# Sorted block attention and an affine MLP on one core: k mixed in four row tiles, the Sinkhorn steps dealt differently, x written by blocks on three queues, W2 loads moved, the last output tile in column halves

## The chip, the cores and the metric

The kernel runs on one core of one Trainium2 chip. The metric is the time of one execution in device microseconds (us). The kernel before ran three times: 330.39, 331.08 and 332.67 us, median 331.08 us.

## The reference

There are two stages. The first is an attention within blocks, whose keys and values are first mixed over blocks by a matrix P that comes from a Sinkhorn iteration; the second is a residual MLP.

```python
# q, k, v: (4, 8, 768, 64); sort_net: (4, 8, 8, 8); a block has 96 rows
P = sort_net
for _ in range(5):
    P = P - np.max(P, axis=-1, keepdims=True)
    P = np.exp(P)
    P = P / (np.sum(P, axis=-1, keepdims=True) + 1e-09)
    P = P / (np.sum(P, axis=-2, keepdims=True) + 1e-09)
k_sorted = np.einsum('bhij,bhjcd->bhicd', P, k_b)     # the same for v
scores = scale * np.matmul(q_b, k_sb.transpose(0, 1, 2, 4, 3))
attn = softmax(scores)
x = heads_side_by_side(np.matmul(attn, v_sb))         # (4, 768, 512)

a1 = alpha1 * x + beta1
tok = np.einsum('ts,bsd->btd', w_tok, a1)
u = x + lam * tok
a2 = alpha2 * u + beta2
out = u + lam * (np.maximum(a2 @ w_ch1, 0.0) @ w_ch2) # hidden size 2048
```

## The kernel before

The four batches go through attention and then through the MLP. The order of all instructions on every engine is the order in which the Python code emits them (a manual schedule); each engine takes its own in that order, and semaphores hold it where data or a buffer is missing. The interleaving is done by generators: each `yield` gives a cost, and `run(gen, n)` lets a generator emit n more pieces.

PSUM is two pools, `psS` and `psM`, of two buffers each. A buffer that is still to be read is not given out again, so where one of the two is held, the other serves alone.

**Front.** `sinkhorn(0)` normalises P of batches 0 and 1, `sinkhorn(1)` that of 2 and 3; each iteration is an exp with row sums on ScalarE (ACT), a reciprocal and a product on VectorE (DVE), a matmul for the column sums on TensorE (PE, L197) into a psS buffer, and again a reciprocal and a product. `big_p` turns P into the weights of the mixing matmuls (L222 to L228). `q_path(b)` transposes q on PE (L360) and copies it out (L369). `mix_k(b)` makes the mixed and transposed k: one small matmul for each of the 96 rows of a block and each group of heads (L265). In batches 0 and 1 a matmul uses 32 of the array's rows and 64 of its columns, and two row groups take turns; in batches 2 and 3, which are done together, it uses 64 rows. Every 32 matmuls fill one PSUM tile, which `evict_k` copies out on ACT (L240) or DVE (L242).

**Attention of a batch.** `scores_max` computes the scores once for the row maxima (PE L393, DVE L399), transposes the maxima (L413) and spreads them on a diagonal Dt (L418). `heads` computes the scores again with the maximum taken off (L436, L444), the exp ET on ACT (L451), the product with v (L461), and the normalised rows in `xnat` on DVE (L470, L471). `bounce` writes x to `xscr` in DRAM, one half of the rows (four blocks) at a time, and `read` reads it back as `x16` with token rows in the partitions:

```python
        def bounce(g):
            t0 = g * S // 2
            n = BLK // NT
            dst = xscr[b, t0:t0 + S // 2].rearrange("(i s k) c -> k s i c", s=n, k=NT)
            for kk in range(NT):
                eng = nc.scalar if b == 0 and g == 1 and kk % 2 else nc.sync
                eng.dma_start(dst[kk], xnat[kk * n:(kk + 1) * n, g * 4:(g + 1) * 4])
```

**MLP of a batch.** `tok_mix` has six token tiles; each has six matmuls of 128 x 512 (L531), a product on DVE (L537), an add to u on GpSimd (POOL; for odd tiles of batch 0 on DVE, L539) and a cast to bf16 on ACT (L543). `u_transposes` turns three tiles of u on PE (L559) and scales them into `a2T` on ACT (L568) and DVE (L573). `ch1` is the first channel matmul (L588, eight per step), with a relu on ACT (L598) or DVE (L596); `ch2` the second (L607), with a product on DVE (L614), an add on POOL (DVE for the last batch, L616) and the write of the output from SyncE (SP, L617).

**Order between the two.** Batch 0's attention runs alone; then `mixing()` emits the MLP of all batches, and between its pieces the loop at the end of the code lets `attention()` emit pieces of the later batches, as long as a credit lasts that each MLP piece adds to. POOL's queue issues the loads of q, k, v and the weights (`load_q`, `load_halves`, `load_23`, `load_w1`, `load_w2`). The second half of W1 is held back by a small copy, the gate (L717), until batch 0's second x16 is there. SP's queue issues the writes and reads of x, v and the output.

Of the kernel before, what the change touches and what calls it, by code (L numbers as in the profile page):

```python
# [9 lines left out]
FT = mybir.dt.float32  # L10
# [9 lines left out]
def kernel(  # L20
# [160 lines left out]
    def sinkhorn(n):  # L181
        P = sortP[n]
        rs = wt([128, 1], FT, f"rs{n}")
        c8 = wt([128, NB], FT, f"c8{n}")

        top = wt([128, 1], FT, f"top{n}")
        nc.vector.tensor_reduce(top[:], P[:], AXX, ALU.max, negate=True)
        for it in range(5):
            if it == 0:
                nc.scalar.activation(P[:], P[:], AF.Exp, bias=top[:], accum_out=rs[:])  # L190
            else:
                nc.scalar.activation(P[:], P[:], AF.Exp, accum_out=rs[:])
            yield
            nc.vector.reciprocal(rs[:], rs[:])
            nc.vector.tensor_scalar(P[:], P[:], rs[:], None, op0=ALU.mult)
            cs = ps2(psS)
            nc.tensor.matmul(cs[:, 0, 0:NB], blkf, P[:], start=True, stop=True)  # L197
            yield
            if it == 0:

                nc.vector.tensor_scalar(c8[:], cs[:, 0, 0:NB], 1e-9, None, op0=ALU.add)
                nc.vector.reciprocal(c8[:], c8[:])
            else:
                nc.vector.reciprocal(c8[:], cs[:, 0, 0:NB])
            nc.vector.tensor_tensor(P[:], P[:], c8[:], ALU.mult)

        BD = BD_of[n] = wt([128, 16, NB], F16, f"BD{n}")
        nc.vector.tensor_tensor(
            BD[:], P[:].unsqueeze(1).to_broadcast([128, 16, NB]),
            mask_blk[:].unsqueeze(2).to_broadcast([128, 16, NB]), ALU.mult,  # L210
        )
        yield
# [20 lines left out]
    def kT_tile(b):  # L233

        kT_of[b] = at([128, H4 * NB, BLK], F16, "kT", 2)

    def evict_k(b, cols, t16):
        dst = kT_of[b][:, :, t16 * 16:(t16 + 1) * 16].rearrange("p c (b t) -> p c b t", b=2)
        if t16 % 2 == 0:
            nc.scalar.copy(dst, cols)  # L240
        else:
            nc.vector.tensor_copy(dst, cols)  # L242

    def mix_k(b, pools):
        raw = raw_of["k", b]
        both = (b, b + 1) if b == 2 else (b,)
        for b_ in both:
            kT_tile(b_)
        w = 32 * len(both)
        for t16 in range(BLK // 16):  # L250
            ps = ps2(pools[t16 % len(pools)])
            for turn in range(2):
                for tt in range(8):

                    for hl in range(2):
                        bank = (hl + turn) % 2
                        t = t16 * 16 + bank * 8 + tt
                        if b == 2:
                            r = slice(hl * 64, hl * 64 + 64)
                            P = PT_of[1][r, r]  # L260
                        else:
                            th, t = divmod(t, BLK // 2)
                            r = slice(th * 64 + hl * 32, th * 64 + hl * 32 + 32)
                            P = PT_of["k"][r, b, hl * 32:hl * 32 + 32]
                        nc.tensor.matmul(  # L265
                            ps[hl * 64:hl * 64 + 64, bank, tt * w:(tt + 1) * w],
                            raw[r, t * D:(t + 1) * D], P,
                            start=True, stop=True,
                        )
            cols = ps[:, :, 0:8 * w].rearrange("p b (t c) -> p c b t", c=w)  # L270
            for n, b_ in enumerate(both):
                evict_k(b_, cols[:, n * 32:n * 32 + 32], t16)
            yield 1.2

    def vS_tile(b):
# [104 lines left out]

    D_of = {}

    def scores_max(b):

        mx = at([BLK, 2, H4, NB], FT, "mx", 1)
# [22 lines left out]
        mxf = mx[:].rearrange("p l h i -> p l (h i)")  # L408
        nc.vector.tensor_copy(mh[:, :, 0, :], mxf)
        nc.vector.tensor_tensor(mh[:, :, 1, :], mxf, mh[:, :, 0, :], ALU.subtract)  # L410
        yield 0.6
        tp = psS.tile([128, 2, 1024], BF, name="m_ps", tag="psS")
        nc.tensor.transpose(  # L413
            tp[:, 0, 0:BLK], mh[:].rearrange("p l e c -> p (l e c)"), identbf[0:BLK, 0:BLK]
# [1 line left out]
        for g in range(2):  # L416
# [2 lines left out]
                Dt[:], tp[:, 0, 0:BLK].unsqueeze(1).to_broadcast([128, 4, BLK]),  # L419
                mask_j[:, g * 4:(g + 1) * 4].unsqueeze(2).to_broadcast([128, 4, BLK]), ALU.mult,  # L420
            )
        yield 1.0

    x16_of = {}

    def heads(b, xpool):
# [50 lines left out]
            )  # L477

        def bounce(g):
            t0 = g * S // 2  # L480
            n = BLK // NT
            dst = xscr[b, t0:t0 + S // 2].rearrange("(i s k) c -> k s i c", s=n, k=NT)
            for kk in range(NT):
                eng = nc.scalar if b == 0 and g == 1 and kk % 2 else nc.sync
                eng.dma_start(dst[kk], xnat[kk * n:(kk + 1) * n, g * 4:(g + 1) * 4])

        def read(g):
            t0 = g * S // 2
# [36 lines left out]
    def tok_mix(b):  # L525
        u = u_of[b]
        u16 = u16_of[b] = mt([128, NT, C], BF, "u16", 1)
        for kt in range(NT):
            ps = ps2(psM)
            for ks in range(NT):  # L530
                nc.tensor.matmul(  # L531
                    ps[:, 0, :], w_tokT[ks][:, kt * 128:(kt + 1) * 128],
                    x16_of[b, ks // 3][:, ks % 3, :],
                    start=(ks == 0), stop=(ks == NT - 1),
                )
            tmp = mt([128, C], FT, "tmp", 2)
            nc.vector.tensor_tensor(tmp[:], ps[:, 0, :], a1lB[:], ALU.mult)  # L537
            eng = nc.vector if b == 0 and kt % 2 else nc.gpsimd
            eng.tensor_tensor(u[:, kt], u[:, kt], tmp[:], ALU.add)  # L539
            if b == 0 and kt < 3:  # L540
                add_x0(kt + 3)
            if kt > 0:
                nc.scalar.copy(u16[:, kt - 1], u[:, kt - 1])  # L543
            if b == 0 and kt > 0:
                load_w2(kt - 1)
            if kt == NT - 2:
                u_transposes(b, 0, psM if b == 0 else psS)
            yield 1.0
        nc.scalar.copy(u16[:, NT - 1], u[:, NT - 1])

    def u_transposes(b, half, pool):
# [49 lines left out]
    def ch2(b, half, k1):  # L601

        u, hT = u_of[b], hT_of[b, half]
        kt = half * 3 + k1
        ps = ps2(psM)
        for m in range(HT):
            nc.tensor.matmul(  # L607
                ps[:, 0, :], hT[m // 2][:, m % 2, k1 * 128:(k1 + 1) * 128],
                W2[:, m, :], start=(m == 0), stop=(m == HT - 1),
            )  # L610
            if m == HT // 2 - 1:
                yield 1.8
        tmp = mt([128, C], FT, "tmp", 2)
        nc.vector.tensor_tensor(tmp[:], ps[:, 0, :], lamB[:], ALU.mult)  # L614
        eng = nc.vector if b == B - 1 else nc.gpsimd
        eng.tensor_tensor(u[:, kt], u[:, kt], tmp[:], ALU.add)  # L616
        nc.sync.dma_start(out[b, kt * 128:(kt + 1) * 128, :], u[:, kt])  # L617
        yield 1.8

    def tok_weights():  # L620
# [38 lines left out]


    vS_tile(0)
    sink, sink1, q0 = sinkhorn(0), sinkhorn(1), q_path(0, psS)
    run(sink, 4)
    nc.scalar.copy(ident16[:], ident32[:])
    run(sink1, 1)
    for it in range(3):
        run(sink, 1)
        run(sink1, 1)
        run(sink, 1)
        if it == 0:  # L670
            nc.scalar.copy(identbf[:], ident32[:])
        if it == 1:
            nc.vector.tensor_reduce(
                m4[:], mask_blk[:].rearrange("p (g h) -> p h g", h=H4), AXX, ALU.add
            )
            nc.scalar.activation(
                nsel[:], m4[:].unsqueeze(2).to_broadcast([128, H4, BLK]), AF.Identity, scale=-1.0
            )
        if it < 2:
            run(sink1, 1)  # L680
# [1 line left out]
    run(sink)  # L682
    big_p(0)
    run(q0, 1)
    mk0 = mix_k(0, [psM, psS])
    for n in range(6):
        run(mk0, 1)
        run(sink1, 1)
        if n == 0 or n == 2:
            run(q0, 1)  # L690
    run(q0)
    run(mk0)
    run(sink1)
    big_p(1)
    load_halves("k", k, 1)
    load_q(1)
    load_w1(0)
# [1 line left out]
        nc.gpsimd.tensor_tensor(dst[:], src[:], lamB[:], ALU.mult)  # L699

    top, mix, tokw = scores_max(0), mix_v0(psM), tok_weights()
    for _ in range(8):
        run(top, 1)
        run(mix, 1)
    run(top, 1)
    run(tokw, 2)
    run(top)
# [14 lines left out]

    def attention():
        yield from mix_v1(psS)
        yield from mix_k(1, [psS])
        yield from q_path(1, psS)
        yield from scores_max(1)
        yield from heads(1, psS)
        yield from mix_v23(psS)
        yield from mix_k(2, [psS])  # L730
        yield from q_path(2, psS)
        load_q(3)
        yield from scores_max(2)
# [3 lines left out]
        yield from heads(3, psS)  # L737

    att_ = attention()
    run(att_, 8)  # L740
    for kt in range(3):
        add_x0(kt)
    run(att_, 6)


    def mixing():

        for _ in tok_mix(0):
            yield 1.0
        for b in range(B):  # L750
            part = ch1(b, 0)
            yield next(part)
# [27 lines left out]
    for part in mixing():  # L780
        credit = min(credit + part, 3.0)
        while credit > 0.0:
            cost = next(att_, None)
            if cost is None:
                break
            credit -= cost
    run(att_)


# [28 lines left out]
```

## Time and profile before

| | |
|---|---|
| runs | 330.39, 331.08, 332.67 us |
| profiled execution: its own time | 333.6 us |
| profiled execution: span of its instructions | 331.8 us |
| mean granted TensorE clock | 0.963 |
| PE busy | 299.9 us (90%), 2926 matmuls |
| DVE, ACT, POOL busy | 156.0, 122.4, 100.6 us |
| L588 and L607 (the two channel matmuls) | 89.1 and 88.6 us |
| L531 (token mixing) | 36.3 us |

All durations come from the profiled execution; the span is what its instructions cover, and 1.8 us of its own time lie around that. A busy PE is not a PE at its peak, since matmuls overlap and the clock that the throttle grants can be half. "Idle before" in brackets at the end of a timeline row tells how long the engine waited and for whom. POOLq, SPq and ACTq stand for the issue of DMAs by those engines' queues.

### The profile page before, as it was taken

How to read it: one execution, taken by the hardware profiler on the slowest of the kernel's cores; microseconds unless marked ns; L12 is line 12 of the kernel's file. 1: busy time of each engine (PE TensorE's matmuls, PEld its weight loads, DVE VectorE, ACT ScalarE, POOL GpSimd, SP SyncE). 2: the span in 40 equal slices, each digit the busy share in tenths (PEclk: the TensorE clock that was granted, in tenths of full speed). 3: DMA queues.
4: the chain of work that ended last, by engine and by line, in shares of the span. 5: the costliest groups of instructions: out<-in, count | busy, mean ns of one | idle time of the engine just before them, and what ended most of it. 6: DMA issues, size and time to landing. Idle time of an engine off the chain costs nothing.

```text
span 331.8 us, 6817 instructions
## 1 busy us (share of the span) xinstructions
PE 299.9 (90%) x2926; PEld 177.7 (54%) x2926; DVE 156.0 (47%) x290; ACT 122.4 (37%) x190; POOL 100.6 (30%) x103
## 2 busy tenths in 40 slices
PE   2579888897899999987999999999999999999994
PEld 2469775743465456443566446645554545554641
DVE  5447663577645444863546844452111153123223
ACT  4324583313584265142354026342220524220400
POOL 8207100238221191641110118073204763300000
PEclk9999995587999999997999999999999999999999
DMA  7998926999999579900035013203101000101001
GB/s 104 200 216 200 207 38 149 204 162 148 222 213 171 129 302 137 152 1 32 34 81 145 3 62 79 49 5 125 63 2 63 33 2 32 63 2 63 32 34 63
DMA packets 39170, 33.35 MB, mean 101 GB/s; under 512 B 20836, under 2 KB 33892, under 8 KB 38692
## 3 DMA queue, kind: packets, MB, share of 16 engines
q0 software_dynamic: 9552, 15.60, 26.6%
q1 hardware_dynamic: 29348, 17.12, 22.7%
q8 instruction: 23, 0.38, 0.5%
q10 hardware_dynamic: 240, 0.20, 0.3%
q14 instruction: 7, 0.06, 0.1%
HBM read 35.93 MB, written 11.80 MB: 144 GB/s over the span
## 4 chain that ended last, share of the span: by engine, by line
PE 75%; DVE 9%; DMA 5%; ACT 4%; POOL 3%; issue 2%; DVEq 0%; ACTq 0%; POOLq 0%; SPq 0%
PE psM L607 25%; PE psM L588 24%; PE psM L531 4%; PE psS L461 3%; DMA W<-in_moe_w_ch_dram 3%; POOL u L539 3%; PE psS L436 3%; DVE mx L399 2%; PE psS L393 2%; PE q_ps L360 2%; PE psS L265 2%; DVE tmp L537 2%; PE psS L444 2%; ACT ET L451 1%; PE uT_ps L559 1%
## 5 line engine op out<-in xcount | busy, mean ns | idle before, releaser
L588 PE MATMUL psM<-a2T,W 128*128 128x384 bf16 x512 | 89.1, 326 | 0.4 <-ACT hT L598 0.3
L607 PE MATMUL psM<-W,hT 128*128 128x512 bf16 x384 | 88.6, 384 | 0.0
L598 ACT ACTIVATE hT<-psM 128x768 bf16<-128x768 f32 x48 | 38.9, 811 | 73.6 <-PE psM L588 73.5
L588 PEld LDWEIGHTS <-W 128*128 128x128 bf16 x512 | 48.2, 98 | 31.4 <-issue 0.7
L607 PEld LDWEIGHTS <-hT 128*128 128x128 bf16 x384 | 37.0, 99 | 42.2 <-issue 1.7
L616 POOL TENSOR_TENSOR u<-u,tmp 128x512 f32<-128x512 f32 x18 | 22.8, 1264 | 95.1 <-DVE tmp L614 95.1
L451 ACT ACTIVATE ET<-psS 96x768 f16<-96x768 f32 x32 | 25.5, 804 | 34.5 <-PE psS L444 34.1
L614 DVE TENSOR_TENSOR tmp<-psM,lamB 128x512 f32<-128x512 f32 x24 | 16.6, 691 | 43.9 <-PE psM L607 43.4
L539 POOL TENSOR_TENSOR u<-u,tmp 128x512 f32<-128x512 f32 x21 | 27.4, 1309 | 31.7 <-DVE tmp L537 31.6
L596 DVE TENSOR_SCALAR hT<-psM 128x768 bf16<-128x768 f32 x16 | 15.3, 957 | 45.2 <-PE psM L588 45.2
L531 PE MATMUL psM<-x,w_tokT 128*128 128x512 f16 x144 | 36.3, 400 | 0.2 <-DVE tmp L537 0.2
L399 DVE TENSOR_REDUCE mx<-psS 96x8 f32<-96x768 f32 x32 | 29.9, 948 | 4.7 <-PE psS L393 4.3
L543 ACT CAST u<-u 128x512 bf16<-128x512 f32 x20 | 12.3, 617 | 30.6 <-POOL u L539 29.7
L531 PEld LDWEIGHTS <-w_tokT 128*128 128x128 f16 x144 | 13.5, 101 | 15.8 <-issue 2.6
L537 DVE TENSOR_TENSOR tmp<-psM,a1lB 128x512 f32<-128x512 f32 x24 | 16.5, 688 | 11.1 <-PE psM L531 11.0
L515 POOL TENSOR_TENSOR u<-x,rb 128x1024 f32<-128x1024 f16 (+1 forms) x12 | 19.3, 1637 | 0.0
L393 PE MATMUL psS<-kT,qT 64*96 64x96 f16 x256 | 14.8, 233 | 2.5 <-ACT a2T L568 1.6
L471 DVE TENSOR_TENSOR xnat<-psS,recip 96x512 f16<-96x512 f32 x24 | 16.5, 686 | 1.2 <-DVE recip L470 0.3
L393 PEld LDWEIGHTS <-qT 64*96 64x96 f16 x256 | 11.1, 136 | 10.7 <-issue 9.3
L461 PEld LDWEIGHTS <-ET 96*96 96x96 f16 x256 | 14.1, 124 | 4.2 <-ACT ET L451 2.2
L470 DVE RECIPROCAL recip<-psS 96x8 f32<-96x8 f32 x24 | 4.9, 204 | 24.2 <-PE psS L461 24.2
L265 PEld LDWEIGHTS <-raw 32*64 32x64 f16 (+1 forms) x576 | 14.3, 137 | 3.2 <-issue 3.1
(102 smaller groups left out, 290.3 us busy)
## 6 DMA issues: line engine op xcount, KB each, us to landing
out_dram<-u SPq DMA_DIRECT2D x24, 256.0 KB, 2.0
qn<-in_q_dram POOLq DMA_DIRECT2D x16, 192.0 KB, 6.7
raw<-in_k_dram POOLq DMA_DIRECT2D x8, 384.0 KB, 11.3
x<-xscr SPq DMA_DIRECT2D x8, 384.0 KB, 3.6
xscr<-xnat SPq DMA_DIRECT2D x45, 64.0 KB, 2.1
raw<-in_v_dram POOLq DMA_DIRECT2D x6, 384.0 KB, 12.7
W<-in_moe_w_ch_dram POOLq DMA_DIRECT2D x2, 1024.0 KB, 11.7
W<-in_moe_w_ch_dram POOLq DMA_DIRECT2D x4, 512.0 KB, 8.2
```

What stands on the lines that cost most here:

```text
L265: nc.tensor.matmul(ps[hl * 64:hl * 64 + 64, bank, tt * w:(tt + 1) * w], raw[r, t * D:(t + 1) * D], P, start=True, stop=True,)
L393: nc.tensor.matmul(sp[0:BLK, hl, i1 * BLK:(i1 + 1) * BLK], qT_of[b, h4][r, i * BLK:(i + 1) * BLK], kT_of[b][r, h4 * 8 + i, :], start=True, ...
L399: nc.vector.tensor_reduce(mx[:, :, h4, g * 4:(g + 1) * 4], sp[0:BLK, :, 0:4 * BLK].rearrange("p l (i t) -> p l i t", t=BLK), AXX, ALU.max,)
L451: nc.scalar.activation(ET[:].rearrange("p l i s -> p l (i s)"), sp[0:BLK, :, 0:4 * BLK], AF.Exp, scale=scale,)
L461: nc.tensor.matmul(xp[0:BLK, hl, i1 * VP:i1 * VP + D + 1], ETs[n][:, hl, i1, :], vS_of[b][:, hl * 32 + h4 * 8 + g * 4 + i1, 0:D + 1], star ...
L531: nc.tensor.matmul(ps[:, 0, :], w_tokT[ks][:, kt * 128:(kt + 1) * 128], x16_of[b, ks // 3][:, ks % 3, :], start=(ks == 0), stop=(ks == NT ...
L537: nc.vector.tensor_tensor(tmp[:], ps[:, 0, :], a1lB[:], ALU.mult)
L539: eng.tensor_tensor(u[:, kt], u[:, kt], tmp[:], ALU.add)
L588: nc.tensor.matmul(ps[:, m1, 0:384], W1[:, ci, m * 128:(m + 1) * 128], a2T_of[b, half, ci][:], start=(ci == 0), stop=(ci == CT - 1),)
L598: nc.scalar.activation(t_[:], ps[:, :, 0:384], AF.Relu)
L607: nc.tensor.matmul(ps[:, 0, :], hT[m // 2][:, m % 2, k1 * 128:(k1 + 1) * 128], W2[:, m, :], start=(m == 0), stop=(m == HT - 1),)
L616: eng.tensor_tensor(u[:, kt], u[:, kt], tmp[:], ALU.add)
```

## The change

- The k mix of batches 0 and 1 has three rounds of 64 matmuls in place of six of 32. Four row groups take turns, and the two halves of the block rows go to a psM and a psS tile, each copied out as before, one on ACT and one on DVE. Batches 2 and 3 keep their matmuls (`mix_k23`).
- The Sinkhorn generator yields once more, between the product and the matmul, so that its pieces can be dealt one by one. The rest of the second chain and its `big_p(1)` move behind the k mix, in between the pieces of `scores_max(0)`. Batch 0's q transposes use psM.
- `bounce` writes one block per DMA (four for each half, on 96 partitions, in an order of 6 x 16 rows); in batch 0's second half they are issued by SP (two), ACT and POOL.
- The four W2 loads are issued together ahead of token mixing. All u adds of `tok_mix` are on POOL. Batch 0's first `u_transposes` comes after token mixing; for later batches the next token tile follows the transposes at once.
- Before token mixing of batch 0, the attention of batch 1 emits seven pieces in place of fourteen, so that its q transposes lie between the token tiles. The last two pieces of `scores_max` end an attention turn (`END`).
- The last output tile is computed, scaled and written in two column halves, the second write from ACT's queue.

```diff
             nc.vector.tensor_scalar(P[:], P[:], rs[:], None, op0=ALU.mult)
+            yield
             cs = ps2(psS)
...
+    def mix_k(b):
+        raw, PK = raw_of["k", b], PT_of["k"]
+        kT_tile(b)
+        for rnd in range(3):
+            ps = ps2(psM), ps2(psS)
+            for turn in range(2):
+                for tt in range(8):
+                    for th in range(2):
+                        for hl in range(2):
+                            bank = (hl + turn) % 2
+                            t = rnd * 16 + bank * 8 + tt
+                            r = slice(th * 64 + hl * 32, th * 64 + hl * 32 + 32)
+                            nc.tensor.matmul(
+                                ps[th][hl * 64:hl * 64 + 64, bank, tt * 32:(tt + 1) * 32],
+                                raw[r, t * D:(t + 1) * D], PK[r, b, hl * 32:hl * 32 + 32],
+                                start=True, stop=True,
+                            )
+            for th in range(2):
+                cols = ps[th][:, :, 0:256].rearrange("p b (t c) -> p c b t", c=32)
+                evict_k(
+                    b, cols, th * (BLK // 2) + rnd * 16,
+                    nc.vector.tensor_copy if th else nc.scalar.copy,
+                )
+            yield 2.4
...
-        yield 0.6
+        yield END                       # END = 9.0, after the maxima
...
-        yield 1.0
+        yield END                       # after Dt
...
-            for kk in range(NT):
-                eng = nc.scalar if b == 0 and g == 1 and kk % 2 else nc.sync
-                eng.dma_start(dst[kk], xnat[kk * n:(kk + 1) * n, g * 4:(g + 1) * 4])
+            for i in range(g * 4, g * 4 + 4):
+                eng = nc.sync
+                if b == 0 and g == 1 and i > 5:
+                    eng = nc.scalar if i == 6 else nc.gpsimd
+                eng.dma_start(
+                    xscr[b, i * BLK:(i + 1) * BLK].rearrange("(s k) c -> k s c", k=NT),
+                    xnat[:, i],
+                )
...
-            eng = nc.vector if b == 0 and kt % 2 else nc.gpsimd
-            eng.tensor_tensor(u[:, kt], u[:, kt], tmp[:], ALU.add)
+            nc.gpsimd.tensor_tensor(u[:, kt], u[:, kt], tmp[:], ALU.add)
...
-            if b == 0 and kt > 0:
-                load_w2(kt - 1)
-            if kt == NT - 2:
-                u_transposes(b, 0, psM if b == 0 else psS)
-            yield 1.0
+            if kt == NT - 2 and b > 0:
+                u_transposes(b, 0, psS)
+            else:
+                yield 2.0 if kt == NT - 1 and b > 0 else 1.0
...
+        last = b == B - 1 and kt == NT - 1
+        for n in range(2 if last else 1):
+            c = slice(n * 256, n * 256 + 256) if last else slice(0, C)
+            for m in range(HT):
+                nc.tensor.matmul(
+                    ps[:, n, 0:c.stop - c.start], hT[m // 2][:, m % 2, k1 * 128:(k1 + 1) * 128],
+                    W2[:, m, c], start=(m == 0), stop=(m == HT - 1),
+                )
...
+            (nc.scalar if n else nc.sync).dma_start(
+                out[b, kt * 128:(kt + 1) * 128, c], u[:, kt, c]
+            )
...
-    sink, sink1, q0 = sinkhorn(0), sinkhorn(1), q_path(0, psS)
+    sink, sink1, q0 = sinkhorn(0), sinkhorn(1), q_path(0, psM)
...
-    mk0 = mix_k(0, [psM, psS])
-    for n in range(6):
-        run(mk0, 1)
-        run(sink1, 1)
-        if n == 0 or n == 2:
-            run(q0, 1)
-    run(q0)
-    run(mk0)
-    run(sink1)
-    big_p(1)
+    mk0 = mix_k(0)
+    run(mk0, 1)
+    run(sink1, 1)
+    run(q0, 1)
+    run(sink1, 1)
+    run(mk0, 1)
+    run(sink1, 1)
+    run(q0)
+    run(sink1, 1)
+    run(mk0)
+    run(sink1, 1)
...
-    for _ in range(8):
+    for n in range(8):
         run(top, 1)
         run(mix, 1)
+        if n == 0 or n == 2:
+            run(sink1, 1)
+        if n == 4:
+            big_p(1)
...
     att_ = attention()
-    run(att_, 8)
+    for n in range(4):
+        load_w2(n)
+    run(att_, 6)
     for kt in range(3):
         add_x0(kt)
-    run(att_, 6)
+    run(att_, 1)
...
         for _ in tok_mix(0):
             yield 1.0
+        u_transposes(0, 0, psM)
+        yield 1.0
...
-            credit -= cost
+            credit = credit - cost if cost < END else 0.0
```

## The prediction

> **What bounds the kernel now.** I read the windows view first, ten microseconds a row; columns are PE, PEld, DVE, ACT, POOL busy time, then the granted clock (1.00 is full), DMA share and GB/s.
>
> ```profile
> 0.00:10.00 10.00, 3.08 (x12) 2.83 (x12) 5.75 (x31) 4.42 (x17) 8.17 (x18) 1.00 0.79 115
> ...
> 40.00:50.00 10.00, 8.89 (x154) 7.12 (x151) 5.87 (x14) 8.46 (x12) 0.00 (x0) 1.00 0.37 67
> 50.00:60.00 10.00, 8.55 (x205) 6.32 (x206) 3.77 (x8) 3.15 (x4) 0.37 (x2) 0.55 0.73 179
> 60.00:70.00 10.00, 9.10 (x127) 5.64 (x123) 5.88 (x10) 2.18 (x3) 3.08 (x4) 0.59 1.08 175
> 70.00:80.00 10.00, 7.57 (x64) 3.84 (x61) 9.14 (x15) 4.05 (x7) 6.31 (x7) 0.92 1.24 138
> ...
> 150.00:160.00 10.00, 8.22 (x64) 4.11 (x63) 3.52 (x9) 2.73 (x4) 1.27 (x1) 0.83 0.08 28
> ```
>
> From 90 us on PE is busy in nearly every row, so only work that PE drops or its few gaps can shorten the kernel there (140 to 160 and 180 to 200). Before 90 us PE waits on serial chains, or runs at half clock (0.55, 0.59). There the change can win. Second, the timeline of the front:
>
> ```profile
> 14.18 0.27 PE L222 MATMUL p_ps<-ident,BD 64*64 64x64 f16 x4 [0.89 <-ACT qT L369]
> ...
> 14.78 0.26 PE L226 MATMUL p_ps<-ident,BD 128*128 128x128 f16 x1 [0.33 <-DVE PK L224]
> ...
> 15.40 0.85 PE L360 MATMUL q_ps<-ident,qn 128*64 128x128 f16 x12 [0.35 <-ACT PT L228]
> ...
> 16.18 1.03 PE L265 MATMUL psM<-PK,raw 32*64 32x32 f16 x32
> ```
>
> The brackets show q tiles and P transposes passing one psS buffer to each other (the other holds a Sinkhorn sum of chain 1). L360's 12 transposes take 0.85 here and 0.53 at 129.00, so PE is really at half clock although the row says 1.00; the k mix at 16.18 is too. Third, the chain of waits and the timeline around the return of x and the first MLP tile:
>
> ```profile
> 51.42 2.46 DMA xscr<-xnat
> 53.90 1.94 DMA xscr<-xnat
> 55.92 3.66 DMA x<-xscr
> ```
>
> ```profile
> 65.43 2.74 PE L531 MATMUL psM<-x,w_tokT 128*128 128x512 f16 x6
> ...
> 68.41 1.47 PE L531 MATMUL psM<-x,w_tokT 128*128 128x512 f16 x6
> ...
> 82.25 1.47 PE L588 MATMUL psM<-a2T,W 128*128 128x384 bf16 x8
> ...
> 88.27 1.46 PE L588 MATMUL psM<-a2T,W 128*128 128x384 bf16 x8
> ```
>
> x is back at 59.58, but token mixing (L531) starts at 65.43, behind the k mix and four q tiles; dense work starts at 88.27. Fourth, batch 1's token mixing, with two PE stalls and its q loads on POOL:
>
> ```profile
> 131.70 1.45 POOL L130 DMA_DIRECT2D qn<-in_q_dram  x2 [7.18 <-PE q_ps L360]
> ```
>
> ```profile
> 144.41 0.38 PE L393 MATMUL psS<-kT,qT 64*96 64x96 f16 x8 [1.60 <-ACT a2T L568]
> ...
> 151.79 0.36 PE L436 MATMUL psS<-Dt,nsel 64*96 64x384 bf16 x2 [1.27 <-DVE Dt L418]
> ```
>
> **The change, part by part.**
>
> *q in psM, k mix in four row tiles (to the first scores, 27.83 before).* The p_ps transposes no longer wait for the q copy: BD is ready at 12.83 and 12 transposes (0.85) end at 12.9, so they run at 12.95 and not 14.18, the second after PK's copy at 13.6, the next q tile at 13.85 to 14.65, and the mix starts at 14.65 instead of 16.18. The mix now: 32 matmuls are 16 pairs side by side, (1.03 - 0.21 for the last one) / 15 = 55 ns a pair. Four at once have no row. Bounds: nothing gained (64 in 1.92 us) or four in the time of two (16 x 0.055 + 0.15 = 0.95 us a round). Each pair already overlaps fully in other rows, and the four go to four banks, so I take 0.95. Copies per round, 0.59 on ACT and 0.69 on DVE, lie beside each other and are shorter. Round 0 ends 15.6; q tile to 16.4; round 1 to 17.4; a Sinkhorn matmul (its DVE input is ready at 17.75) to 18.4; q tile to 19.2; round 2 to 20.1; ACT first waits for the Sinkhorn product (20.25), does its exp (0.4) and then the copy (0.6): 21.3. Gain 6.5.
>
> *Sinkhorn's rest, moved into the scores.* Before, eight maxima pass DVE at 1.0 us each, with two psS buffers. Now a Sinkhorn sum holds one buffer over two maxima: each costs a scores matmul (0.58) and a handover more, 2 x 0.65 = 1.3. Reciprocal, product and BD (0.21 + 0.17 + 0.29 and gaps) cost 0.85 on DVE, big_p(1)'s buffer some 0.5. Loss 2.6, so the first softmax exp comes 6.5 - 2.6 = **3.9** earlier. PE's order from there to the last x block is unchanged.
>
> *From the last x block (51.39, call it E) to dense work (88.27, E + 36.9).* The bounce issues 4 writes of 96 KB per half in place of 6 of 64 KB. Bounds for x's return (8.2 before): one issue 0.4 + 2.1 (the median write) + 3.66 = 6.2; the slowest write 5.2 + 0.8 + 3.66 = 9.7. I keep 8.2, the nearest row. ACT issues one DMA (0.4) and not three (2.1), so mix_v1's first copy starts about 1.1 sooner; the mix of k then takes 3 x 0.95 and PE is free at E + 6.1 (E + 10.0 before). The first token tile needs x: done at E + 9.5, not E + 16.7. Then, q tiles now lying between: 24 transposes 1.6; tile 1 at half clock 2.6; q 0.8; tile 2 2.6 (I leave it cold: the transposes at 61.4 to 65.4 did not bring the clock); q 0.45; three tiles with scores, 3 x 1.71, and 0.3; u transposes 0.8: E + 23.8. But ACT's a2T copies now stand behind u16's last cast, and that behind POOL, which does all six u adds (1.27 each, two on the row of 1.70): last tmp E + 23.5, add 1.3, cast 0.6, two a2T 1.2: first L588 at E + 26.6 (E + 30.9 before). Two L588 groups 2.8, two scores 0.6, transposes 0.6, 0.4 owed to attention: dense at E + 31.0. Gain **5.9**. POOL's seven issues behind the gate (W1, two columns, four W2 x 0.78) take 5.5, to E + 13.7, and the first add waits for them; its tmp is there at E + 10.3, so that wait costs POOL 3.4, which the last add no longer sees because POOL needs 1.3 per tile of 1.7. W2 landed at 87.4 before, 14 us ahead of use; issued earlier it stays hidden. DVE loses three adds of 0.69 in its 9.14 row.
>
> *Batch 1, token mixing.* L393 no longer stands between transposes and tile 5, which hides most of the 1.60 wait; END puts a ch2 step between the maxima and Dt, which hides 1.27 and 0.5 behind it. But load_q(3)'s four issues (0.73 each, 2.9) now stand ahead of u add 2 on POOL, where they ended before the first add at 136.28. Add 2 ends 1.8 later than the transposes want it, and scores in pairs add a 0.9 wait on DVE. Idle 3.0 against 3.7; and if the half-clock stretch (3.25 for an L607 of 1.73 at 153.93) goes, 1.5 more. Bounds 0.7 and 2.2; I take **1.4**. Batch 2's gap (PE 18.64 of 20 in 180 to 200): **1.0** of 1.36.
>
> *Last tile in halves.* After the last matmul stand 0.69 + 0.69 on DVE and a write. Half the columns: about 0.35 each; **0.7** saved. 16 more matmuls hide their weight loads (99 ns) behind 256 columns (0.216 / 2 = 108 ns); uncovered they would cost under 0.3.
>
> Sum: 3.9 + 5.9 + 1.4 + 1.0 + 0.7 = 12.9. The profiled execution took 333.6 (span 331.8), so 320.7 for it; the runs' median is 331.1, so **318.2**.
>
> A rule speaks against the bounce. The Trainium skill ("DMA: Bandwidth & Descriptors", section "Why a DMA increments its semaphore by 16 and not by 1") says a DMA is spread over the largest number of engines up to 16 that divides the slowest dimension of both sides. The old write has 16 and 16, the new one 6 and 96: six engines, 16 KB each and all four writes on the same ones. By its 27 GiB/s that is an estimated 0.6 us a write, 2.4 a half in place of 0.9; x would come about 1.5 later and the sum be 11.4. No write of before has such a shape.
>
> And the Trainium skill ("TensorE: Matmul & The Clock Gate", Part 1) has the clock fall after an idle window of about 3.4 us. The 0.55 row has PE 8.55 busy, with matmuls of 32 x 64 tiles: here busy alone did not keep it. By the rule alone tiles 1 and 2 would be warm and the sum 2.4 larger.
>
> **Rivals.**
> - *x returns late* (chance 0.14). The second half's writes queue behind a slow one of the first: 0.8 + 5.2 + 2.1 + 3.66, x at E + 11.8 and not E + 8.2, and all after it 3.6 later: 321.8. For it: nothing hides this read. Against: the median write is 2.1.
> - *Four tiles run as two* (0.12). Front 3 x 0.95 = 2.9 less, the later mix about 1.5: 322.6.
> - *The clock* (0.15, of it 0.09 in whole), the slower end. The wT transposes bring full clock just before the softmax of batch 0 (the 40 to 50 row). Shifted in time, they may miss it: PE's 8.9 us in that row double at worst, +8.9; tiles 3 to 5, two L588 groups and the scores at half clock add 3 x 1.3 + 2 x 1.2 = 6.3. Together 15.2, more than the 12.9: 333.4. It decides once full clock is not granted before the first L588. Against: only dense products are needed, and they come earlier.
>
> **How the numbers follow.** The forecast has 0.59. Own range 314 to 322.5. The range reaches down to 311, where x is early (2.0 more), batch 1 at its upper bound (0.8), tiles 1 and 2 at full clock (2.4) and the k mixes too (L265 at 118.03 has 33 ns a pair, so 6 x 16 x 0.022 = 2.0), and up to 327, into the part-cold cases, leaving two in ten out. About 1% (3.3 us) is what a measurement tells from no change. Faster 0.85: forecast, late x, two tiles; same 0.06 and slower 0.09 from part and whole of the clock case.
>
> **What would show it.** Right: 64 matmuls of the mix in about 0.95; first scores near 21.3; first token tile within 10 us of the last x block; first ch1 group 26 to 27 us after it; no wait for Dt near 140; one 0.35 pair at the end. Wrong: x landing beyond E + 10, a clock of 0.5 in the batch 0 softmax, W2 awaited by the first ch2, or a longer wait for u16 in batch 1.

## Result and the profile after

The change made the kernel slower: 341.98 us (median of four runs, 339.65 to 342.98) against 331.08 (median of three, 330.39 to 332.67), a ratio of 1.031 with a 95% interval of 1.023 to 1.039. A fourth run of the kernel before, 337.31 us, fell in a slower state and is left out of this ratio. The forecast was 318.2 us, 3.9% below the kernel before. The profiled execution took 342.98 us, its span 341.2.

The windows of the kernel after (columns PE, PEld, DVE, ACT, POOL busy, granted clock, DMA share, GB/s):

```profile
40.00:50.00 10.00, 9.50 (x178) 7.58 (x175) 7.28 (x17) 6.21 (x8) 0.70 (x1) 1.00 0.20 52
50.00:60.00 10.00, 6.63 (x202) 3.63 (x201) 5.42 (x8) 3.73 (x5) 1.13 (x3) 0.54 0.61 177
60.00:70.00 10.00, 9.34 (x86) 4.82 (x86) 7.54 (x10) 2.83 (x5) 8.54 (x9) 0.78 1.10 174
70.00:80.00 10.00, 7.53 (x79) 4.15 (x77) 6.95 (x10) 4.33 (x8) 7.25 (x10) 1.00 1.43 223
80.00:90.00 10.00, 7.99 (x81) 4.61 (x75) 5.03 (x9) 7.50 (x12) 2.67 (x4) 1.00 1.08 204
90.00:100.00 10.00, 0.00 (x0) 0.00 (x0) 0.00 (x0) 0.53 (x1) 0.71 (x1) 0.59 1.35 195
100.00:110.00 10.00, 6.83 (x46) 3.94 (x48) 1.89 (x5) 2.72 (x4) 0.00 (x0) 0.56 0.13 17
...
150.00:160.00 10.00, 7.79 (x77) 4.07 (x76) 6.99 (x10) 4.11 (x7) 8.03 (x9) 1.00 0.77 97
```

One row tells the result: from 90 to 100 us PE does nothing at all, while the DMA engines are full. The next row has the half clock (0.56) that follows. The chain of waits names the cause (start, duration, what):

```profile
56.90 4.94 DMA vscr<-raw
...
61.91 41.13 DMA vS<-vscr
...
103.17 0.82 PE psS L482 x8
103.99 2.56 PE psM L609 x8
```

This is the transfer that brings batch 1's mixed v back from DRAM as vS (L348 after, L329 before). I call it the gather. In the kernel before it was issued at 62.4 and took 17.3 us:

```profile
L329 SPq DMA_DIRECT2D vS<-vscr x1: 328/328/328, 62.4 to 62.4; - x1
...
DMA to landing us min/median/max: 17.3/17.3/17.3
```

So it landed at 79.7, was needed at 92.0, and nothing waited. After, it takes 41.1 us, and the values of batch 1 (L482) wait for it for 14.4 us:

```profile
103.17 0.82 PE L482 MATMUL psS<-vS,ET 96*96 96x65 f16 x8 [14.44 <-DMA vS<-vscr]
```

Until then the change did most of what it was meant to do. The first fence below is the front; the second has the first token tile, the first channel matmuls and the first dense ones:

```profile
12.89 0.27 PE L223 MATMUL p_ps<-ident,BD 64*64 64x64 f16 x4
...
13.68 0.85 PE L379 MATMUL q_ps<-ident,qn 128*64 128x128 f16 x12
...
20.78 0.18 PE L255 MATMUL psS<-PK,raw 32*64 32x32 f16 x1 [1.53 <-issue]
...
22.33 0.56 PE L414 MATMUL psS<-kT,qT 64*96 64x96 f16 x8 [0.82 <-DVE kT L240]
```

```profile
58.80 1.44 PE L554 MATMUL psM<-x,w_tokT 128*128 128x512 f16 x3 [0.92 <-DMA x<-xscr]
76.69 1.46 PE L609 MATMUL psM<-a2T,W 128*128 128x384 bf16 x8 [2.33 <-ACT a2T L589]
...
81.55 1.46 PE L609 MATMUL psM<-a2T,W 128*128 128x384 bf16 x8
```

First scores are at 22.33 (27.83 before), the last x block at 48.89 (51.39), dense work at 81.55 (88.27): 6.7 us ahead of before. The 14.4 us at L482 and the half clock after it take all of this back and more. Later:

```profile
150.14 2.89 POOL L130 DMA_DIRECT2D qn<-in_q_dram  x4
```

```profile
155.04 0.73 PE L580 MATMUL uT_ps<-identbf,u 128*128 128x128 bf16 x10 [1.73 <-ACT u L565]
...
163.81 0.50 PE L580 MATMUL uT_ps<-identbf,u 128*128 128x128 bf16 x6 [0.96 <-DVE mx L420]
```

```profile
335.34 1.91 PE L631 MATMUL psM<-W,hT 128*128 128x256 bf16 x16 [0.52 <-DVE tmp L638]
```

The q loads stand between the u adds, as foreseen; the wait for Dt is gone, and so is the half-clock stretch (0.83 in the row of 150 to 160 before; after, every row from 110 to 200 has 1.00). The last line is new: the second column half waits for DVE's read of the first.

### The profile page after: what moved, and what is told of

Read it like the earlier page. It is cut to its first block, busy times and chain, and to the rows that moved or that the text cites. A ratio compares the mean times of both kernels' runs of the same rounds, so it can differ in the third digit from the quotient of the medians.

```text
span 341.2 us, 6820 instructions
## 1 busy us (share of the span) xinstructions
PE 293.9 (86%) x2927; PEld 174.1 (51%) x2942; DVE 156.3 (46%) x289; ACT 122.1 (36%) x190; POOL 104.6 (31%) x107
## 4 chain that ended last, share of the span: by engine, by line
PE 69%; DMA 14%; DVE 6%; ACT 4%; POOL 3%; issue 2%; ACTq 0%; SPq 0%; DVEq 0%; POOLq 0%
PE psM L631 23%; PE psM L609 23%; DMA vS<-vscr 12%; PE psS L482 3%; PE psM L554 3%; PE psS L457 3%; POOL u L561 3%; PE psS L414 2%; PE psS L465 2%; DVE mx L420 2%; DMA vscr<-raw 1%; PE q_ps L379 1%; PE psS L198 1%; PE wT_ps L650 1%; PE psM L482 1%
## 5 line engine op out<-in xcount | busy, mean ns | idle before, releaser
L609 PE MATMUL psM<-a2T,W 128*128 128x384 bf16 x512 | 91.0, 331 | 2.8 <-ACT a2T L589 2.3
L631 PE MATMUL psM<-W,hT 128*128 128x512 bf16 (+1 forms) x385 | 85.5, 371 | 1.6 <-DVE tmp L638 0.5
L631 PEld LDWEIGHTS <-hT 128*128 128x128 bf16 x400 | 38.0, 98 | 40.6 <-issue 0.7
L640 POOL TENSOR_TENSOR u<-u,tmp 128x512 f32<-128x512 f32 x18 | 22.7, 1263 | 106.1 <-DVE tmp L638 102.0
L561 POOL TENSOR_TENSOR u<-u,tmp 128x512 f32<-128x512 f32 x24 | 30.8, 1297 | 31.9 <-DVE tmp L560 31.8
L638 DVE TENSOR_TENSOR tmp<-psM,lamB 128x512 f32<-128x512 f32 (+1 forms) x25 | 16.8, 670 | 43.0 <-PE psM L631 42.1
L482 PE MATMUL psS<-vS,ET 96*96 96x65 f16 x192 | 13.6, 217 | 15.7 <-DMA vS<-vscr 14.4
L482 PEld LDWEIGHTS <-ET 96*96 96x96 f16 x256 | 14.8, 129 | 18.7 <-issue 14.5
L414 PE MATMUL psS<-kT,qT 64*96 64x96 f16 x256 | 13.5, 230 | 3.5 <-DVE mx L420 1.1
L414 PEld LDWEIGHTS <-qT 64*96 64x96 f16 x256 | 10.6, 135 | 10.7 <-issue 9.4
```

Of the source, the lines that this page charges most:

```text
L414: nc.tensor.matmul(sp[0:BLK, hl, i1 * BLK:(i1 + 1) * BLK], qT_of[b, h4][r, i * BLK:(i + 1) * BLK], kT_of[b][r, h4 * 8 + i, :], start=True, ...
L482: nc.tensor.matmul(xp[0:BLK, hl, i1 * VP:i1 * VP + D + 1], ETs[n][:, hl, i1, :], vS_of[b][:, hl * 32 + h4 * 8 + g * 4 + i1, 0:D + 1], star ...
L561: nc.gpsimd.tensor_tensor(u[:, kt], u[:, kt], tmp[:], ALU.add)
L609: nc.tensor.matmul(ps[:, m1, 0:384], W1[:, ci, m * 128:(m + 1) * 128], a2T_of[b, half, ci][:], start=(ci == 0), stop=(ci == CT - 1),)
L631: nc.tensor.matmul(ps[:, n, 0:c.stop - c.start], hT[m // 2][:, m % 2, k1 * 128:(k1 + 1) * 128], W2[:, m, c], start=(m == 0), stop=(m == HT ...
L638: nc.vector.tensor_tensor(tmp[:, c], ps[:, n, 0:c.stop - c.start], lamB[:, c], ALU.mult)
```

## Why the gather is slow: what the transfers show

The gather is 768 KB in packets of 128 bytes, 6144 of them, on SP's queue. (A packet here is one record of a transfer in the trace.) Beside it runs POOL's queue. POOL's timeline, first of before, then of after:

```profile
59.75 0.81 POOL L643 DMA_DIRECT2D W<-in_moe_w_ch_dram  x1
...
70.63 0.77 POOL L649 DMA_DIRECT2D W<-in_moe_w_ch_dram  x1
...
80.26 2.00 POOL L116 DMA_DIRECT2D raw<-in_v_dram  x4
```

```profile
59.05 0.77 POOL L669 DMA_DIRECT2D W<-in_moe_w_ch_dram  x1
...
61.29 3.02 POOL L675 DMA_DIRECT2D W<-in_moe_w_ch_dram  x4
...
74.79 2.04 POOL L116 DMA_DIRECT2D raw<-in_v_dram  x4
```

Before, W2 was issued from 70.6 on, one load per token tile. After, all four loads are issued at 61.3 to 64.3, behind half of W1, and the v and k loads follow at 74.8. POOL's queue is hardly ever empty from 59 to about 102 us. The transfers by queue (q0 is POOL's, q1 SP's; packets, MB, share): the first fence is before from 68 to 72 us, the others are after, from 68 to 78 and from 80 to 92.

```profile
q1 hardware_dynamic: 4184, 0.54, 145.1%
q0 software_dynamic: 70, 0.07, 10.8%
```

```profile
q0 software_dynamic: 1838, 1.84, 110.7%
q1 hardware_dynamic: 1837, 0.24, 29.3%
```

```profile
q0 software_dynamic: 326, 2.47, 100.2%
q1 hardware_dynamic: 326, 0.04, 8.9%
```

Where both queues have work, they pass one packet each: 1838 to 1837, 326 to 326. So the gather's speed is set by the size of the other queue's packets. Beside W2's 1-KB packets it gets 184 packets a us (1837 in 10 us), beside the v and k loads 27 (326 in 12 us; 199 of POOL's 326 packets there have 12 KB, most others 4 bytes), and in a pause of POOL's queue 1046 (4184 in 4 us). Before, two thirds of it passed in a pause of 4 us between the last packets of W1's second half and the first of W2. The early W2 loads filled that pause. The Trainium skill ("DMA: Bandwidth & Descriptors", section "Queues, rings and completion order") says that each DMA engine goes round-robin between the queues at packet granularity, a packet being typically some 9 to 17 descriptors. The counts here agree with the turns, one record of the trace to one; whether such a record is a packet in that sense, no run here shows.

## The experiments

Theory G: W2's early place costs the time, because the gather gets through only in a pause of POOL's queue. Rivals: the gather is slow by itself; the wait is put down to the wrong transfer; W2 itself is late; the other parts of the change cost it.

**W2 early in the kernel before.**

```diff
 # kernel before, ahead of attention()
+    for n in range(4):
+        load_w2(n)
 # tok_mix
-            if b == 0 and kt > 0:
-                load_w2(kt - 1)
```

> The kernel before with one edit: the four W2 loads are issued together behind the gate, as the change has them. Theory G: the gather lands at 100 to 105 us in place of 79.7 us, L461 waits for it from about 92 us on, 9 to 13 us, with 2 us of half clock behind that: 340 to 347 us. Rival R: within 1% of 331 us.

344.97 us, ratio 1.040 (1.033 to 1.048). The gather took 36.1 us (issued 63.9) and the values waited for it:

```profile
L461 PE MATMUL psS<-vS,ET x40: 210/210/287, 100.2 to 111.6; 96*96 96x65 f16 x40
...
  DMA vS<-vscr: 8.7, 1
```

This one edit, without anything else of the change, makes the kernel before slower by at least as much as the whole change did (1.040 against 1.031).

**W2 back into token mixing in the kernel after** (the reverse edit).

> The changed kernel, but the four W2 loads are issued where the kernel before had them, between the u adds of batch 0's token mixing. Theory G (the gather queues behind loads): batch 1's gather of v (vS<-vscr, 128-byte packets on SP's queue) gets one small packet for each large packet of POOL's queue, and W2 issued early leaves that queue no pause until 103 us. Then the gather lands by about 82 us, the wait of 14.4 us before L482 is gone, the half-clock stretch behind it too (some 2.5 us), and the time is about 325 us. Rival R (the wait has another cause: the v writes, the new order on PE, the clock): L482 still waits over 10 us and the time stays near 342 us.

342.22 us, ratio 1.034 (1.028 to 1.041): G's number missed by 17 us. L482 still waits 14.0 us. The timeline of POOL tells why: token mixing runs earlier now, so its W2 loads are issued at 65.0, 67.0, 69.1 and 71.1, before W1's second half has landed (near 70.4), and the v loads follow at 73.1. The loads were put back in the program, but only a short pause came back: 1422 of the gather's 6144 packets pass between 67 and 69, and from 70 to 80 it again gets some 190 a us. It is the pause that counts, not the place of W2 as such.

**The same with the old x writes.**

```diff
 # kernel after with W2 back in token mixing; bounce(g):
-            for i in range(g * 4, g * 4 + 4): ...
+            for kk in range(NT): ...        # as in the kernel before
```

> As e1_w2_back, and x is written as before (six writes of 64 KB a half, on SP and ACT). If the writes by blocks hold x back: batch 0's second x16 lands 8 to 8.5 us after the last x block (10.0 in the changed kernel), the first ch1 group and the end come 1.5 us earlier than in e1: about 323.5 us. Rival: POOL's chain of issues and adds sets that stage whatever x does, and the time is that of e1 within 0.5 us.

Four runs: 327.55, 328.11, 337.78 and 338.62 us; the lower two give a ratio of 0.990 (0.981 to 0.999). Neither of the numbers expected came. The profiled execution is the one of 337.78: POOL's queue had a pause from 66 to 71 in which 5159 of the gather's 6144 packets passed, but the last of them crawled, first behind W2, then behind the v and k loads (21 packets from 82 to 95, beside 340 of POOL's); it landed at 98.2 and L482 waited 8.9 us. That what is left over at the end sits on few of the 16 engines would fit 21 packets beside 340, but the trace doesn't name the engines. That the two runs near 328 caught the pause whole would fit as well, but no profile of them was taken.

**The v, k and q loads later in the program.**

```diff
 # kernel after, mixing(), batch 0
-                load_23("v", v); load_23("k", k); load_q(2)     # behind u_transposes(0, 1)
...
+                load_23("v", v); load_23("k", k); load_q(2)     # behind ch1(0, 0)
```

> The changed kernel with W2 early as it is, but the loads of v, k and q for batches 2 and 3 are issued behind the first ch1 half instead of after its second group. Theory G: POOL's queue is empty from about 84 us, the gather then goes through in 2 to 4 us and lands at 85 to 88 us, about when L482 needs it: a wait under 1 us and about 325 us. Rival (W2's bytes alone delay the gather, the later loads don't matter): it lands after 95 us, L482 waits over 6 us, and the time is over 333 us.

341.52 us, ratio 1.033 (1.025 to 1.040), a wait of 12.1 us. The edit didn't do what it was for: POOL has nothing to do or to wait for between the two places, so the v loads were issued at 74.28 in place of 74.79. It tells nothing of G. To hold a queue back takes data to wait for, not a later line.

**A gate on the gather.**

```diff
 # kernel after
-    for n in range(4):
-        load_w2(n)
     run(att_, 6)
...
         for _ in tok_mix(0):
             yield 1.0
+        gate2 = wt([1, 2], F16, "gate2")
+        nc.gpsimd.tensor_copy(gate2[:], vS_of[1][0:1, 0, 0:2])
+        for n in range(4):
+            load_w2(n)
```

> Kernel after, with the four W2 loads taken out of their early place and put behind batch 0's token mixing, where GpSimd first copies two elements of batch 1's gathered vS: no W2 or v/k load can then be issued before the vS gather (L348) has landed. Theory G (the gather's 128-byte packets share the DMA engines packet for packet with whatever GpSimd's queue is carrying, and get through only in a pause of that queue): the gather, issued near 61.6, lands near 72 to 77 instead of 103; the scores' values (L482) wait for it no longer; the time is 321 to 327 us. Rival R1 (the gather is slow by itself, for instance by the form of its destination): it still takes about 40 us, and the time stays near 342, or above because W2 is later still. Rival R2 (the gather is mended, but W2, now issued near 75 and needed by L631 near 95, is late in its place): no wait at L482, a wait at L631 for W2, 328 to 335 us.

325.67 us (325.26 to 328.55), ratio 0.987 (0.974 to 0.999). POOL's timeline:

```profile
70.69 1.26 POOL L561 TENSOR_TENSOR u<-u,tmp 128x512 f32<-128x512 f32 x1 [0.27 <-DVE tmp L560]
76.56 0.17 POOL L782 COPY gate<-vS 1x2 f16<-1x2 f16 x1 [4.61 <-DMA vS<-vscr]
77.04 3.00 POOL L675 DMA_DIRECT2D W<-in_moe_w_ch_dram  x4 [0.32 <-PE psS L414]
```

The gather, issued at 62.0, landed by 76.6 in place of 103, and L482 waits for it no more. W2, now issued at 77, is not waited for at its first use (92.3). The same computation with one copy of two elements and the same loads issued later is 16.3 us faster than the kernel after. So G stands; that the gather is slow by itself, that the wait was put down to the wrong transfer and that W2 is late are ruled out. Against the kernel before, the gain is 1.3%, and the interval nearly reaches 1.

**The gate and the old x writes.**

> The same gate, and besides x written as the kernel before wrote it (per position in token tiles, on two queues). If the block writes on three queues cost what the trace suggested (x back at E+9.9 with them, against a little over E+9 with the old ones), this is 0 to 1.5 us below the gated kernel with block writes; if the block writes were a gain of their own as predicted (1.2 us), it is that much above. Theory G also expects its runs to agree with each other, unlike the ungated kernel with old writes, whose runs fell near 328 and near 338: 322 to 326 in all of them.

324.84 us (323.63 to 325.83), ratio 0.981 (0.972 to 0.991): its runs agree, where those of the ungated kernel with these writes lay near 328 and near 338. The two ways of writing x differ by less than these runs can tell, so neither the gain of 1.2 us that the expectation allows the block writes nor a loss by them is shown in the whole time.

**The gate in the kernel before.**

> Kernel before with nothing but the gate: W2 loads taken out of batch 0's token mixing and put behind it and behind the copy from the gathered vS. Theory G: the gather already passes in a pause of GpSimd's queue there (issued 62.4, landed 79.7, needed at 92), so the time stays within 1% of the kernel before (328 to 333 us); the gather lands a little earlier, near 72 to 76. If it becomes faster by more than 1%, the gather or the loads cost the kernel before something that its profile did not show; if slower by more than 1%, the gate costs something by itself (W2 or the v loads late), which then has to be taken off the other two results.

332.83 us (328.93 to 333.72), ratio 1.002 (0.996 to 1.008). The gather takes 13.7 us in place of 17.3 and nothing comes of it, as it wasn't waited for. So the gate costs nothing that shows (within 1%), and the gain of the gated kernels belongs to the rest of the change.

**Two PSUM tiles for the last halves, and the q loads of batch 3 out of the u adds' way.**

```diff
 # gate and old x writes, ch2
-        ps = ps2(psM)
         for n in range(2 if last else 1):
+            ps = ps2(psM)
 # attention(): load_q(3) out; mixing(), behind tok_mix(1):
+            if b == 0:
+                load_q(3)
```

> Gate and old x writes as in the kernel before it, and two more edits: the two column halves of the last tile go to two PSUM tiles instead of two banks of one, and load_q(3)'s four issues on GpSimd stand behind batch 1's token mixing instead of ahead of its second u add. If the halves' gain of 0.7 us was lost to the wait of the second half's matmuls for the first half's read (0.52 us at L629), 0.5 us of it comes back and no such wait is shown. If the four issues (2.9 us) hold the u adds of batch 1 as read, the transposes there come 1 to 2 us earlier. Together 1 to 2.5 us below gate and old writes: 322.3 to 323.8 against 324.8. Rival: the u adds' delay is covered by attention's work on TensorE, and only the 0.5 us of the tail shows (324.3).

324.21 us (321.77 to 325.53), ratio 0.975 (0.966 to 0.984): the fastest median, but not to be told from 324.84 by these runs. Its timeline shows both edits doing their work; the wait of 0.52 us at L629 (L631 of after) is gone, and the 12 transposes run without the wait of 1.73:

```profile
138.00 1.02 PE L578 MATMUL uT_ps<-identbf,u 128*128 128x128 bf16 x12
```

```profile
314.71 4.95 PE L629 MATMUL psM<-W,hT 128*128 128x512 bf16 x38
```

From the third ch1 group to the end of the span it takes 240.7 us, against 242.9 without the two edits and 243.5 in the kernel before. In this profiled execution the half clock lasted longer around the first ch1 groups (granted clock 0.968 over the whole span, 0.979 in the other), which hides it in the total.

**END taken back.**

```diff
 # gate and old x writes
-        yield END          # both
+        yield 0.6          # and 1.0
...
-            credit = credit - cost if cost < END else 0.0
+            credit -= cost
```

> Gate and old x writes as before it, and the rule that deals attention's steps out between the MLP's put back as it was (the two steps of the maxima cost 0.6 and 1.0, no END). The prediction gave END 1.0 us at batch 2's maxima and a part of 1.4 at batch 1's (the Dt wait of 1.27 us). If that was right the time rises by 1 to 2 us, to 326 to 327. Rival: the trace of the gated kernels shows as much idle time of TensorE from the first dense work to the end as before (12.6 us against 10.7), so END only moved the holes: 324 to 325.5, no change.

327.58 us (327.17 to 327.86), 2.7 above the kernel with END; ratio to before 0.988 (0.981 to 0.994). No run of one kernel reaches the other's, though the intervals of the two ratios overlap; from the third ch1 group to the end the profiled executions take 245.2 and 242.9. The sum is what END was priced at (1.0 at batch 2, 1.27 and 0.5 at batch 1), but in part by luck, as the waits stand elsewhere. Near 150, where the 1.27 stood before, this kernel has only 0.30, for the maxima; it waits 1.17 for batch 1's Dt at 85.3, which the prediction didn't price, and 1.21 for batch 2's maxima at 186.5 (0.43 with END). The rival, read from sums of idle time, fell: a sum over 240 us doesn't tell what one wait costs.

**Sixteen more matmuls ahead of the hole.**

```diff
 # gate and old x writes, mix_k
-                for tt in range(8):
+                for tt in ([0, 1, 2, 3] if b == 0 and rnd + turn == 0 else []) + list(range(8)):
```

> Gate and old x writes as before it, with the first 16 matmuls of batch 0's k mix issued twice (same results written again). It asks what the hole of 1.53 us on TensorE inside the mix's second round (19.25 to 20.78, charged to nothing) hangs on. If on the place in TensorE's instruction stream, the hole comes 16 matmuls earlier in the mix: after about 9 of the second round's 64 and not after 25. If on the second round itself or on what runs beside it, it stays after about 25. If it hangs on none of these it is gone. In each case the mix is 0.25 to 0.5 us longer.

325.39 us in one run. The timeline of PE in the last of the mix's three rounds (the expectation counts them from nought):

```profile
18.97 0.23 PE L255 MATMUL psM<-PK,raw 32*64 32x32 f16 x2
18.97 0.23 PE L255 MATMUL psS<-PK,raw 32*64 32x32 f16 x2
19.04 0.21 PE L255 MATMUL psM<-PK,raw 32*64 32x32 f16 x2
19.05 0.21 PE L255 MATMUL psS<-PK,raw 32*64 32x32 f16 x1
20.78 0.18 PE L255 MATMUL psS<-PK,raw 32*64 32x32 f16 x1 [1.53 <-issue]
```

Seven matmuls of the round are recorded ahead of the hole, 23 in the kernel after: it comes 16 matmuls earlier in the mix, with the same 1.53 us. So it doesn't hang on what the mix does there. It begins at the same time in both kernels, though, so this run alone can't tell a place in PE's instruction stream from a moment. The profiled execution of the gated kernel can: its mix ran 0.47 us later, and so did the hole, after the same 23 matmuls:

```profile
19.51 0.21 PE L255 MATMUL psS<-PK,raw 32*64 32x32 f16 x1
21.24 0.18 PE L255 MATMUL psS<-PK,raw 32*64 32x32 f16 x1 [1.52 <-issue]
```

So it belongs to a place in PE's instruction stream.

## Why the prediction was wrong

**The step that failed** is the one on W2: "W2 landed at 87.4 before, 14 us ahead of use; issued earlier it stays hidden." That is true of W2 and priced only W2. What W2's loads now run beside was put at nothing: the gather isn't named in the prediction at all. It lay in the same stretch, with 12 us to spare, and the trace of before held what was needed: most of its 17.3 us passed in a pause of POOL's queue, which ended with the first W2 load. In its place the runs show 17.7 us of span (341.2 against 323.5 with the gate): 14.4 of wait, 1.3 by which the fifth ch1 group is already late (84.91 and 83.58), and the rest at half clock behind the wait. Of the 1.3 the trace shows two possible sources, which no run separates: POOL issues the four W2 loads ahead of its first u add, which starts at 64.26 and not at 60.97, and the second token tile runs at half clock (2.74 us and not 1.47). None of the rivals had it. The clock rival as written didn't come (full clock in batch 0's softmax, the row of 40 to 50), nor did four tiles run as two (the first round took 0.97 us up to the next instruction).

The other steps, by the gated kernel (325.26 in its profiled execution, 323.5 span), where 8.3 of the predicted 12.9 us arrived between the two profiled executions (by all runs it is less, 1.3%, or some 4 us):

- *Front, 3.9 predicted, 2.2 to 2.7 measured.* The four row tiles were right (64 matmuls in 0.97 us, 0.95 predicted; the sum written there, 16 x 0.055 + 0.15, makes 1.03), the Sinkhorn steps cost 2.8 (2.6). What was missing is the hole of 1.53 us on PE in the third round, which no row of before showed. Taking it off the measured 22.33, first scores would be at 20.8 (21.3 predicted).
- *From the last x block (E) to dense work, 5.9 predicted.* With the gate dense work starts at E + 31.0 (49.21 and 80.2), as forecast, but by luck, as errors cancel: x came back at E + 9.2 and not 8.2; the second token tile, counted cold at 2.6, took 1.47, and the first ch1 group came at E + 24.6 and not 26.6; that group then ran at half clock for most of its 2.44 us. In the other kernels with the gate it was E + 31.5 to 34.1, in the kernel after E + 32.7.
- *Batch 1's token mixing, batch 2's gap and the tail, 3.1 together.* With the gate, 0.2 arrived (243.3 us from dense work to the end, 243.5 before). The q loads' stall took what END gave, and the tail's 0.7 went into the wait of the second half and into DVE steps of 0.42 and not 0.35. With both mended, 2.8 arrived. So the gains were priced about rightly in sum, if not place by place (see END above), and the losses too low: the second half needs a PSUM tile of its own.
- *The return of x.* It came at E + 9.9 in the kernel after and not at 8.2, which the prediction kept because it took 2.1 us for a write. The chain of waits, first of the gated kernel with the block writes, then with the old ones:

```profile
49.99 5.07 DMA xscr<-xnat
55.19 3.22 DMA x<-xscr
```

```profile
51.54 1.92 DMA xscr<-xnat
53.55 6.01 DMA x<-xscr
```

The last write takes 5.07 us and not 2.1. The second read of x is issued at E + 6.0 to 6.2 with the block writes (gated kernel and after), and at E + 4.5 to 4.9 with the old ones (before and the gated kernels): some 1.5 us later, which is what the six-engine rule was worked out to cost. The engines agree with it: SP's queue keeps 36.0% of the 16 engines busy while it writes blocks (46.5 to 49.5 in the kernel after), which is 5.8 of them, and 79.8% with the old writes (48.3 to 51 in the kernel before). So the term was mis-sized, and the rule that spoke against it fits the writes. (One of the four writes of that half goes by POOL's queue; that all four use the same engines, as the prediction has it, no run shows.) But the old writes with the gate lose that again in the read, which takes 4.2 to 6.0 us in place of 3.3 to 3.7, so that x comes at E + 9.2 to 10.7 there. Why the read is slower there was not tried. ACT's one issue took 1.53 us and not 0.4.

## What to carry to other kernels

When a load is moved, look at which small-packet transfers on other queues fall into its new stretch, not only at when it is needed itself. A transfer of 128-byte packets that looks harmless may live on a pause of the queue beside it; let the large loads wait for its data. And a load isn't delayed by a later line in the program unless the engine that issues it has something to wait for, or to do, in between.

## What the runs showed of the hardware that was not expected

- Two busy DMA queues passed one packet each, though one had 128 bytes in it and the other 1 KB or 12 KB: 184 packets of 128 bytes a us beside packets of 1 KB, 27 beside loads with 12 KB, 1046 in a pause.
- PE stops for 1.53 us at one place of its instruction stream, charged to no wait (after 23 matmuls of the third round, at 19.04 in one kernel and 19.51 in another). In the trace of after one instruction packet of 16 KB moves from 18.46 to 19.41, just ahead of it; whether it is what PE waits for was not shown.
- A matmul into the second bank of a two-bank PSUM tile waits for DVE's read of the first (0.52 us); in two tiles it doesn't. Whether the chip asks for that wait or the program's own semaphores do was not shown.
